# Moving the load of x from SyncE's queue to ScalarE's queue at the start of a decode kernel

## The chip, the core and the metric

The kernel runs on one core of a Trainium2 chip. The metric is the device time of one execution in microseconds. Before the change it is 1309.38 us, the median of three runs that lie between 1309.34 and 1309.76 us. The core has a matrix engine (TensorE, PE in the profile), a vector engine (VectorE, DVE), an activation engine (ScalarE, ACT), GpSimd (POOL), and SyncE (SP), which here only issues transfers. ScalarE can issue transfers too. All transfers run on the same 16 DMA engines; what SP issues appears in the profile as queue q1, what ScalarE issues as queue q10.

## The reference

Eight sequences decode one token each. x is 8 x 512. It is normalised to xn, and three things are added: x itself, grouped-query attention of xn over a cache of 8192 keys and values (8 key heads of width 128, 32 query heads), and a two-layer Mish network of xn (512 to 1792 to 512).

```python
xn = layernorm(x)
q = xn @ wq                       # 8 x 32 heads x 128
p = softmax(q . k_cache / sqrt(128))
attention = (p @ v_cache) @ wo
h = xn @ w1 + b1
out = x + attention + (h * tanh(softplus(h))) @ w2
```

All numbers are 32-bit floats. The caches alone are 8 x 8 x 8192 x 128 x 4 bytes each, 537 MB for the two. Each cached number is used once per query head of its group, so the program is mostly a stream from memory.

## The kernel before

The work is cut into 32 units (`UNITS`). A unit is one sequence and two key heads. It loads one block of keys (`kT`, 128 rows of 64 KB, 8.39 MB) and one block of values (`v`, the same size), each with one transfer from `load_unit` (line 145). Four times, once for eight units, the query weights `wq` of two key heads are loaded into `ws` (2 MB) and multiplied with xn (`project`), and the result is spread over a layout that the scores need (`spread`, `key_weights`).

All these blocks live in one large tile `kv`. One place holds values. Two places for keys overlap each other by half. So the transfers depend on what has been read out before them: the next key block may be issued once the first half of the present scores is done, the next value block once the present value products are done.

The scheduling is by hand (`manual_schedule`): each engine executes its instructions in the order in which the program writes them. SP issues nearly all transfers, in the order of the code, and each issue waits until its place is free. What SP has issued runs one after the other on q1.

The start is special in three ways.

- The first key block goes to the value place and has nothing to wait for. It is issued at once, followed by the Mish weights `w1` (line 573).
- The first 2 MB of `wq` are split: SP issues one half (line 159), ScalarE the other (line 160), so both queues work.
- x lies in a corner of `kv` (`x_sb`, line 154) that the second key place will overwrite. It is normalised by a chain of small instructions on VectorE and ScalarE (lines 209 to 225, ending in `xn4`). `project` needs `xn4` and both halves of `ws`. After `spread` and `key_weights`, `x_turn` (lines 248 to 267) reads `x_sb` once more with TensorE (line 252). Only then may SP issue the second key block, kT(1) (line 578 of the code, line 145 in the profile).

After unit 0's scores, SP issues the first value block v(0) (line 603). Then `mish` runs the first Mish layer, whose scratch and weights lie in the other key place; its last VectorE instruction is line 490. Only then may SP issue the third key block, kT(2). Below, kT(j) and v(j) are the blocks of unit j.

ScalarE issues three more small transfers at the start, the bias `b1` (line 165), then loads its table for the square root and takes part in the normalisation.

Of the kernel before, what the change touches and what calls it, by code (L numbers as in the profile page):

```python
# [82 lines left out]
def kernel(  # L83
# [12 lines left out]
    nc = tc.nc  # L96
# [55 lines left out]
    low = kv[:B, LOW_AT : LOW_AT + 3 * D]  # L152
    xe = kv[:B, LOW_AT + 3 * D : LOW_AT + 3 * D + W1R * P].rearrange("b (i s) -> b i s", i=W1R)
    x_sb, xc, sq = (low[:, i * D : (i + 1) * D] for i in range(3))
    nc.sync.dma_start(x_sb, x)  # L155

    rows = wq.rearrange("j p f -> (j p f)").rearrange("(m p f) -> m p f", m=NP, p=P)[0]
    half = CC * BW // 2
    nc.sync.dma_start(ws[:, :half], rows[:, :half])  # L159
    nc.scalar.dma_start(ws[:, half:], rows[:, half:])  # L160
    b1_sb = kv[:G, W1_AT + 7168 : W1_AT + 7168 + FG]

    for lo in range(0, FG, 150):
# [537 lines left out]
```

## Time and profile before

| | before |
|---|---|
| time, median of 3 runs | 1309.38 us |
| span of the profiled execution, first to last instruction | 1307.7 us |
| TensorE busy | 991.8 us (76%) |
| VectorE busy | 357.6 us (27%) |
| ScalarE busy | 39.2 us (3%) |
| moved by the DMA engines | 561.80 MB, mean 430 GB/s |
| of it on ScalarE's queue q10 | 1.06 MB |

The profiled execution's span is the time from its first to its last instruction. It lies 1.7 us under the median of the runs, which are timed from outside and without a profile. An issue row (SPq, ACTq) is the moment at which an engine hands a transfer to the DMA engines; the data moves later. In the rows "idle before <-X" tells how long an engine stood still before an instruction, and what ended that. The DMA view counts the packets that start in a window, by queue; a packet of this program is one contiguous row of a transfer, or a small mark of 4 bytes with which a DMA engine reports that its share is done.

### The profile page before, as it was taken

What the parts mean: (1) busy time and instruction counts of PE and PEld (TensorE: products, weight loads), DVE (VectorE), ACT (ScalarE), POOL (GpSimd) and SP (SyncE); (2) the same over time, 40 slices, a digit from 0 to 9 for tenths busy, and PEclk for the clock granted to TensorE, in tenths of its full rate; (3) what the DMA queues carried; (4) which work ended last, traced back from release to release, by engine and by line L of the source; (5) the groups of instructions that cost most, each with busy time, mean ns of one, the idle gap of its engine ahead of it and who ended that gap; (6) DMA issues with size and microseconds to landing.
All of it is one profiled execution on the core that took longest, in us unless ns stands there. A gap on an engine that the chain in (4) does not pass through costs nothing.

```text
span 1307.7 us, 11247 instructions
## 1 busy us (share of the span) xinstructions
PE 991.8 (76%) x5090; PEld 348.8 (27%) x5090; DVE 357.6 (27%) x676; ACT 39.2 (3%) x89; POOL 2.3 (0%) x10
## 2 busy tenths in 40 slices
PE   6967876768878778776877877687696687777686
PEld 4222222223322222222322222232242222222222
DVE  3352122231233332123221322311323321323321
ACT  1000000000000000000000000000000000000000
POOL 0000000000000000000000000000000000000000
PEclk9999888888888788888888888798888998888898
DMA  9999999999999999999999999999999999999998
GB/s 404 444 421 442 425 439 428 433 435 430 434 433 432 435 432 436 424 442 429 434 434 429 438 425 442 423 440 427 437 426 436 435 428 436 432 432 429 433 435 337
DMA packets 11927, 561.80 MB, mean 430 GB/s; under 512 B 1364, under 2 KB 1632, under 8 KB 2152
## 3 DMA queue, kind: packets, MB, share of 16 engines
q1 hardware_dynamic: 11712, 560.03, 99.2%
q10 hardware_dynamic: 168, 1.06, 0.3%
q8 instruction: 40, 0.66, 0.2%
q14 instruction: 7, 0.06, 0.0%
HBM read 561.01 MB, written 0.07 MB: 429 GB/s over the span
## 4 chain that ended last, share of the span: by engine, by line
DMA 77%; PE 23%; issue 0%; ACT 0%; SPq 0%; DVE 0%
DMA kv<-in_v 57%; DMA kv<-in_kT 18%; PE o L410 15%; PE s L340 7%; DMA kv<-in_w 2%; PE x L379 1%; PE x L304 0%; ACT qr L311 0%; PE o L564 0%; PE m L427 0%; SPq L155 0%; SPq L159 0%; DVE os L661 0%; DVE rt L387 0%; PE m L383 0%
## 5 line engine op out<-in xcount | busy, mean ns | idle before, releaser
L340 PE MATMUL s<-kv,wk 128*64 128x512 f32 x2048 | 502.8, 654 | 177.0 <-DMA kv<-in_kT 169.9
L410 PE MATMUL o<-kv,pt 128*32 128x512 f32 x2048 | 267.6, 682 | 56.6 <-DMA kv<-in_v 56.6
L340 PEld LDWEIGHTS s<-kv,wk 128*64 128x64 f32 x2048 | 164.0, 151 | 492.1 <-issue 403.5
L352 DVE TENSOR_REDUCE nm<-s 128x1 f32<-128x512 f32 x32 | 22.1, 692 | 511.6 <-PE s L340 511.6
L379 PE MATMUL x<-e,perm 128*128 128x512 f32 x256 | 130.7, 658 | 2.0 <-ACT qr L311 2.0
L410 PEld LDWEIGHTS o<-kv,pt 128*32 128x32 f32 x2048 | 70.5, 123 | 227.8 <-issue 175.1
L418 DVE TENSOR_SCALAR os<-o,isel 128x128 f32<-128x128 f32 x32 | 11.2, 351 | 281.5 <-PE o L410 281.5
L390 DVE STREAM_TRANSPOSE tr<-x 128x512 f32<-128x512 f32 x128 | 79.2, 676 | 3.2 <-PE x L379 3.2
L379 PEld LDWEIGHTS x<-e,perm 128*128 128x128 f32 x256 | 50.6, 208 | 75.5 <-issue 72.9
L323 DVE TENSOR_TENSOR wk<-qr,mask 128x1024 f32<-128x1024 f32 (+1 forms) x33 | 62.8, 1902 | 18.8 <-ACT qr L311 18.7
L371 ACT ACTIVATE e<-s,nmx 128x512 f32<-128x512 f32 x32 | 22.0, 687 | 1115.4 <-DVE nmx L368 1115.4
L399 DVE TENSOR_TENSOR pt<-tr 64x512 f32<-64x512 f32 x64 | 43.9, 686 | 1.6
L395 DVE TENSOR_TENSOR tr<-tr 128x1024 f32<-128x1024 f32 x32 | 39.2, 1225 | 1.1
L420 DVE SCALAR_TENSOR_TENSOR os<-o,isel,os 128x128 f32<-128x128 f32 x96 | 33.7, 351 | 3.4
L353 PE MATMUL m<-ident,nm 128*1 128x128 f32 x32 | 8.6, 270 | 25.3 <-DVE nm L352 25.3
L364 PE MATMUL m<-ident,nx 1*128 1x1 f32 x32 | 7.0, 217 | 19.8 <-DVE nx L358 19.8
L304 PE MATMUL x<-qT,tr 128*128 128x64 f32 x128 | 19.3, 315 | 3.0 <-ACT qr L311 2.7
L304 PEld LDWEIGHTS x<-qT,tr 128*128 128x128 f32 x128 | 18.1, 226 | 6.2 <-ACT qr L311 3.3
L353 PEld LDWEIGHTS m<-ident,nm 128*1 128x1 f32 x32 | 2.5, 79 | 53.5 <-DVE nm L352 53.5
L374 DVE TENSOR_SCALAR lsel<-rsel,l 128x8 f32<-128x8 f32 x32 | 7.4, 231 | 28.8 <-ACT e L371 28.8
L427 PE MATMUL m<-hsel,os 128*128 128x8 f32 x64 | 10.9, 242 | 5.6 <-DVE rt L387 5.6
L427 PEld LDWEIGHTS m<-hsel,os 128*128 128x128 f32 x64 | 10.8, 189 | 15.2 <-DVE rt L387 7.2
(107 smaller groups left out, 174.6 us busy)
## 6 DMA issues: line engine op xcount, KB each, us to landing
ws<-in_wq SPq DMA_DIRECT2D x3, 2048.0 KB
kv<-in_wo SPq DMA_DIRECT2D x2, 2048.0 KB
kv<-in_w SPq DMA_DIRECT2D x1, 3584.0 KB
kv<-in_w SPq DMA_DIRECT2D x2, 1024.0 KB
kv<-in_wo SPq DMA_DIRECT2D x1, 1920.0 KB
kv<-in_wo SPq DMA_DIRECT2D x1, 1536.0 KB
ws<-in_wq ACTq DMA_DIRECT2D x1, 1024.0 KB
ws<-in_wq SPq DMA_DIRECT2D x1, 1024.0 KB
```

The source lines that it names most:

```text
L304: nc.tensor.matmul(X[:, half, k * 64 : (k + 1) * 64], wide[:, half * 8 + k], qT, start=True, stop=True,)
L323: nc.vector.tensor_mul(w[:, i : i + n], q[:, i : i + n].to_broadcast([P, n, 2, NH * G, REP]), mask.rearrange("p (o d k r) -> p o d k r", o ...
L340: nc.tensor.matmul(S[64 * c : 64 * (c + 1), :], w[:, i].rearrange("p d k h -> p (d k h)"), kk[:, i, c, :], start=(part == 0 and n == 0), s ...
L352: nc.vector.tensor_reduce(nm, S, axis=AX.X, op=ALU.max, negate=True)
L371: nc.scalar.activation(e, S, AF.Exp, bias=nmx, accum_out=l)
L379: nc.tensor.matmul(X[:, g], perm[:, g], e, start=True, stop=True)
L390: nc.vector.transpose(tr.rearrange("p (l t) c -> p t l c", t=TL)[:, tl], X.rearrange("p g (t q l) -> p t l g q", t=TL, q=PP)[:, tl],)
L395: nc.vector.tensor_add(t[:, :, 0], t[:, :, 0], t[:, :, 1])
L399: nc.vector.tensor_add(pt8[half, :, :, d * REP : (d + 1) * REP].rearrange("p c y h -> p y c h"), t[:, 0], t[:, 1],)
L410: nc.tensor.matmul(O[Q * q : Q * (q + 1), :], pt8[:, c, TL * l : TL * (l + 1), :].rearrange("p t h -> p (t h)"), vt[:, 512 * n : 512 * (n ...
L420: nc.vector.scalar_tensor_tensor(os, O[:, DH * i : DH * (i + 1)], isel[:, i : i + 1], os, op0=ALU.mult, op1=ALU.add)
L427: nc.tensor.matmul(M[:, 168 : 168 + H2], os, hsel, start=True, stop=True)
```

## The change

The issue of x moves from SP to ScalarE. On SP it was the first transfer, ahead of SP's half of `wq`. On ScalarE it comes right behind ScalarE's half of `wq` and ahead of the three pieces of `b1`.

```diff
     x_sb, xc, sq = (low[:, i * D : (i + 1) * D] for i in range(3))
-    nc.sync.dma_start(x_sb, x)
 
     rows = wq.rearrange("j p f -> (j p f)").rearrange("(m p f) -> m p f", m=NP, p=P)[0]
     half = CC * BW // 2
     nc.sync.dma_start(ws[:, :half], rows[:, :half])
     nc.scalar.dma_start(ws[:, half:], rows[:, half:])
+    nc.scalar.dma_start(x_sb, x)
     b1_sb = kv[:G, W1_AT + 7168 : W1_AT + 7168 + FG]
```

The order of SP's issues at the start of the program, as a difference. `ws<-in_wq` is a half of the query weights, `kv<-in_x` is x, `kv<-in_kT` the first key block, `kv<-in_w` the Mish weights. The code loses a line above, so line 159 reads 158 after the change:

```order
 L696 UNCONDITIONAL_BRANCH
-L155 DMA kv<-in_x 8x512
-L159 DMA ws<-in_wq 128x2048
+L158 DMA ws<-in_wq 128x2048
 L145 DMA kv<-in_kT 128x16384
 L573 DMA kv<-in_w 128x7168
```

SP's half of the weights, the first key block and the Mish weights each move one place forward.

The order of ScalarE's issues at the same place (`kv<-in_b` are the pieces of the bias):

```order
 L696 UNCONDITIONAL_BRANCH
-L160 DMA ws<-in_wq 128x2048
+L159 DMA ws<-in_wq 128x2048
+L160 DMA kv<-in_x 8x512
 L165 DMA kv<-in_b 4x150 x2
 L165 DMA kv<-in_b 4x148
```

x stands behind 1 MB on its queue, and the bias and all of ScalarE's later work stand one issue further back. The other engines' instructions and their order are the same.

## The prediction, made before the changed kernel ran

> **What bounds the kernel now.** I read the page first: the busy times and the line of DMA shares in its 40 slices.
>
> ```profile
> span 1307.7 us, 11247 instructions
> PE 991.8 (76%) x5090; PEld 348.8 (27%) x5090; DVE 357.6 (27%) x676; ACT 39.2 (3%) x89; POOL 2.3 (0%) x10
> DMA  9999999999999999999999999999999999999998
> DMA packets 11927, 561.80 MB, mean 430 GB/s; under 512 B 1364, under 2 KB 1632, under 8 KB 2152
> ```
>
> No engine is near full, but the DMA engines are busy in all 40 slices. 561.80 MB at 430 GB/s is 1306 us, the whole span. So only two things change the time: when the stream starts, and whether it ever runs dry.
>
> Next, the chain of waits in order of time (start, duration, what), whose head holds the edited issue.
>
> ```profile
> 0.73 0.38 SPq L155
> 1.11 0.06 issue
> 1.17 0.37 SPq L159
> 1.54 0.04 issue
> 1.59 26.29 DMA kv<-in_kT
> ...
> 44.91 31.03 DMA kv<-in_v
> ```
>
> The reader is to see that x's issue costs SP 0.38 + 0.06 = 0.44 us, that kT(0) lands at 1.59 + 26.29 = 27.88, and that v(0), issued at 44.91, lands only at 75.94. It queues behind other blocks, so the stream has stock. How much stock matters, because the change makes x later.
>
> **The change, part by part.** The timeline of the first microseconds (start, duration, engine and line, in brackets the idle time before):
>
> ```profile
> 0.73 0.38 ACTq L160 DMA_DIRECT2D ws<-in_wq  x1
> 1.15 1.36 ACTq L165 DMA_DIRECT2D kv<-in_b  x3
> 2.43 0.67 DVE L209 TENSOR_REDUCE st<-kv 8x1 f32<-8x512 f32 x1 [0.33 <-DMA kv<-in_x]
> 2.54 1.28 ACT L208 ACT_TABLE_LOAD   x1 [2.54 <-issue]
> 3.31 0.47 DVE L211 TENSOR_SCALAR kv<-kv,st 8x512 f32<-8x512 f32 x1
> 3.94 0.61 ACT L212 ACTIVATE kv<-kv 8x512 f32<-8x512 f32 x1
> 7.26 0.19 DVE L225 COPY xn<-m 128x32 f32<-128x32 f32 x1 [0.80 <-PE m L224]
> 8.66 1.89 PE L279 MATMUL h<-ws,xn 128*8 128x512 f32 x8 [1.44 <-DMA ws<-in_wq]
> 28.01 16.86 PE L340 MATMUL s<-kv,wk 128*64 128x512 f32 x64 [0.58 <-DMA kv<-in_kT]
> ```
>
> *Issues.* SP loses one issue: its half goes out at 0.73 instead of 1.17, and kT(0) and w1 each 0.44 us earlier. ScalarE gains one of about 0.4 us, so the bias and its table load (1.28 us, from 2.54) begin 0.4 us later. That is covered: the table is needed only at L212, which will itself be late. Without the cover it would cost 0.4 us.
>
> *Is the earlier issue on SP worth anything?* The DMA view of two windows, 0 to 4.7 us and then 4.7 to 7.2 us, and of 8.5 to 20 us (queue: packets, MB, share):
>
> ```profile
> q10 hardware_dynamic: 110, 0.90, 61.9%
> q1 hardware_dynamic: 16, 0.02, 1.5%
> ...
> q1 hardware_dynamic: 111, 0.91, 85.7%
> q10 hardware_dynamic: 56, 0.15, 15.4%
> ...
> q1 hardware_dynamic: 77, 5.05, 101.4%
> ```
>
> Until 4.7 us q1 has moved x alone, though SP's half was issued at 1.17; the engines were busy with ScalarE's half, issued at 0.73 before and after. SP's half followed at once. Whichever half goes first, kT(0) begins after the same 2 MB. The gain lies between 0 and the full 0.44 us; I take 0.1, since the engines are served from the other queue meanwhile.
>
> *When does x come?* Before, it was issued at 0.73 and released L209 at 2.43. Now it stands behind 1 MB on q10, and the other half shares the engines. L279 shows that both halves had landed by 8.66. If ScalarE's half goes first alone, x comes one half sooner: 1.05 MB at 430 GB/s is 2.4 us, so at 6.2. If the halves take turns and x follows directly, at about 8.7. Or it meets kT(0) first. In the third window q1 moves 5.05 MB in 77 packets, 65.6 KB each, a whole row of a key block. One of 16 engines moves 430/16 = 26.9 GB/s, so a row holds its engine 2.44 us. The second window shows that the queues mix: bias packets of q10 are moved amid SP's half. If x's row and the mark that reports it take turns with kT(0)'s rows, each turn costs 2.44 us. With n such turns, x comes at R = 8.7 + 2.44 n.
>
> *What R does to the rest.* From L209 to the end of L225 are 7.45 - 2.43 = 5.02 us, and 0.1 less when L212 finds its table ready. L279 then starts at R + 4.95 instead of 8.66, a shift S = R - 3.7: 2.5 us at R = 6.2, 5.0 at n = 0, 7.4 at n = 1, 9.9 at n = 2. From L279 to the first scores (28.01) each engine waits on the one before; the scores start S later, minus the 0.1 us by which the keys were last. Everything queued behind these on PE and DVE moves with them, and two issues of SP behind that:
>
> ```profile
> 27.54 0.34 SPq L145 DMA_DIRECT2D kv<-in_kT  x1
> ...
> 66.99 0.22 DVE L490 COPY aT<-kv 128x112 f32<-128x112 f32 x1
> 67.28 0.33 SPq L145 DMA_DIRECT2D kv<-in_kT  x1
> ...
> 83.20 0.33 SPq L145 DMA_DIRECT2D kv<-in_v  x1
> ...
> 95.34 15.63 PE L340 MATMUL s<-kv,wk 128*64 128x512 f32 x64 [7.69 <-DMA kv<-in_kT]
> ```
>
> *Where the stream could run dry.* SP issues kT(1) at 27.54, once x_turn has read x, and kT(2) at 67.28, once mish has ended (L490). A transfer moves its first bytes about 1.0 us after its issue: x, issued at 0.73, has 8 packets in the window 1.6 to 1.78 us. For the end of v(0), the window 73.8 to 74.5 us:
>
> ```profile
> DMA packets 8, 0.01 MB, mean 68 GB/s; under 512 B 2, under 2 KB 2, under 8 KB 8
> ...
> DMA packets 24, 0.79 MB, mean 1124 GB/s; under 512 B 12, under 2 KB 12, under 8 KB 12
> ```
>
> Twelve of the 16 engines write their closing mark of v(0) there and start on kT(2); the last is done shortly before the landing at 75.94, say 75.4. So kT(2) must be issued between 72.8 and 74.4, and has 5.5 us (first engines) to 7.1 us (last) to spare. kT(1) must come before w1 has drained: 27.88 + 3.67 MB / 430 GB/s = 36.4 landed, about 34.9 as an issue for the last engine, a spare of some 7. v(0), issued at 44.91, follows kT(1), which lands at 36.4 + 19.5 = 55.9, and has over 9. v(1) at 83.20 comes before kT(2) lands (95.34) with over 10. So kT(2) decides, and the loss is about S - 5.5 to S - 7.1, or nothing. A late kT(1) delays v(0) too, so the two losses are not added: the later one sets the sum. Nothing is won back, as the stream has no idle time to give.
>
> *Sum.* R = 6.2 or 8.7: S is 2.5 or 5.0, no loss, -0.1 us. n = 1: S = 7.4, a loss of 0.3 to 1.9. I take the row nearest to the trace, x behind both halves and behind no row or one, and the middle between no loss and the mean of 1.1: +0.5, less the 0.1 at the start, +0.4 us on the profiled span (1308.1) and on the median: **1309.8 us**, with 1309.2 to 1311.3 as this case's own range.
>
> **The rivals.**
>
> *Turns against key rows (slower).* The place is q10 behind ScalarE's half; the price is 2.44 us per turn, and it decides from S = 5.5 to 7.1 on, that is R above 9.2 to 10.8. x and kT(0) are both the second issue of their engine now, so they reach the engines together. n = 2 gives S = 9.9, a loss of 2.8 to 4.4: 1312.2 to 1313.8. n = 3 gives up to 6.8: 1316.2. If SP's half gets ahead, rows of ScalarE's half meet key rows too, and n is 4 to 7: 7.7 to 16.6 us, 1317 to 1326. For it: the mixing in the second window. Against: in the first window one queue's eight packets per engine went without mixing, and if those are ScalarE's again, x escapes.
>
> *A whole block ahead of x.* The first window can be read as each queue being served in long runs. If SP's half, then ScalarE's, then all of kT(0) goes before x, then R = 8.7 + 19.5 = 28.2, S = 24.5, a loss of 17 to 19: 1327 us. The bias that moved amid SP's half speaks against it. The Trainium skill, DMA: Bandwidth & Descriptors, section "Queues, rings and completion order", has this rule: an engine takes a whole packet, typically 9 to 17 descriptors, from one queue before it turns to the next. By it the sum would be 1327 us if SP's half is first and 1309.3 if ScalarE's is. The first window agrees with it, the second does not.
>
> *The full 0.44 us.* If one queue cannot fill the engines at the start, SP's earlier half fills them: 1308.9. Against it stands the 61.9% that q10 took alone, which leaves little, and a late x cannot help.
>
> **How the numbers follow.** The forecast has 0.48, the full gain 0.10, n = 2 or 3 has 0.22, n of 4 to 7 has 0.12, the whole block 0.08. A measurement of this kernel can tell about 0.2%, 2.6 us, from no change. The forecast and nearly all of the gain case lie within it: same 0.56, with 0.02 for faster. The three slow cases lie beyond it: 0.42. The range reaches from the full gain, 1308.9, to n of 3 and the first of 4, 1317, and leaves out 0.2. The forecast's own range is 1309.2 to 1311.3.
>
> **What would show it.** In the changed profile: SP's half issued near 0.73; L209 released by x between 6 and 11 us, L279 five microseconds later and idle on xn instead of on `ws`; the scores of unit 0 at 28.0 + S; kT(2) issued at 67.3 + S. If R is under 9.2, the DMA row stays full through 80 us and the time is the same. If L209 waits until 13 us or more, the forecast is wrong, and windows of the DMA view near 36 and 75 us must show the gap. If R is small and the time still moves by over 2.6 us, the account of the stream is wrong.

## The result, and the profile after

The changed kernel is slower: 1314.43 us, the median of five runs between 1313.03 and 1315.37, against 1309.34 for the kernel before (five runs between 1309.12 and 1309.76). The ratio is 1.0038, with an interval from 1.0027 to 1.0048, a loss of 5.1 us. The profiled execution spans 1311.9 us against 1307.7. That is 4.2 us more; it is one of the faster executions of the changed kernel. The runs of the changed kernel lie 2.3 us apart, those of before 0.6. Two of the ten runs of an experiment below (x behind SP's half) took 1613 us at a granted clock of 0.56 instead of 0.88, and one of 19 runs of the kernel before took 3264 us; the ratios leave these out.

The start of the changed kernel, from its timeline (start, duration, engine and line, in brackets the idle time before and what ended it):

```profile
0.73 0.42 ACTq L159 DMA_DIRECT2D ws<-in_wq  x1
0.73 0.38 SPq L158 DMA_DIRECT2D ws<-in_wq  x1
1.18 0.42 SPq L145 DMA_DIRECT2D kv<-in_kT  x1
1.19 0.58 ACTq L160 DMA_DIRECT2D kv<-in_x  x1
...
13.39 0.68 DVE L209 TENSOR_REDUCE st<-kv 8x1 f32<-8x512 f32 x1 [11.29 <-DMA kv<-in_x]
18.38 1.90 PE L279 MATMUL h<-ws,xn 128*8 128x512 f32 x8 [0.28 <-DVE xn L225]
37.26 0.34 SPq L145 DMA_DIRECT2D kv<-in_kT  x1
...
76.12 0.33 SPq L145 DMA_DIRECT2D kv<-in_kT  x1
```

SP's half and kT(0) are issued 0.4 us earlier, as written. But x, issued at 1.19, releases L209 only at 13.39 instead of 2.43. L279 begins at 18.38 instead of 8.66, now waiting on xn and not on the weights. kT(1) is issued at 37.26 instead of 27.54, and kT(2) at 76.12 instead of 67.28.

Where x waits is seen in the DMA view. The first pair of rows is the window 0 to 8.5 us of the changed kernel, the second pair 8.5 to 13 us (queue: packets, MB, share of the engines):

```profile
q1 hardware_dynamic: 160, 2.10, 66.0%
q10 hardware_dynamic: 144, 1.05, 30.4%
...
q1 hardware_dynamic: 32, 2.10, 107.6%
q10 hardware_dynamic: 16, 0.02, 1.0%
```

By 8.5 us q10 has moved 144 packets, which are the 128 rows and 16 marks of its half, and nothing of x. The 16 packets of the next window are x: eight rows of 2 KB and eight marks. In the same window q1 moves 32 rows of 64 KB, two on each of the 16 engines. The trace has the order: the first rows of kT(0) start from 7.2 us on, x's rows between 9.6 and 10.5, its marks between 12.1 and 13.0. x's data waits for one row of kT(0), x's mark for the next.

What the late issue of kT(1) does is seen microsecond by microsecond (from:to, then the busy time of each engine, the granted clock, the DMA share and GB/s). First before, then after:

```profile
35.00:36.00 1.00, 1.00 (x7) 0.31 (x4) 0.00 (x0) 0.00 (x0) 0.00 (x0) 1.00 2.34 1012
36.00:37.00 1.00, 1.00 (x8) 0.34 (x6) 0.00 (x0) 0.00 (x0) 0.00 (x0) 1.00 0.15 66
37.00:38.00 1.00, 1.00 (x8) 0.44 (x6) 0.00 (x0) 0.00 (x0) 0.00 (x0) 1.00 1.06 459
38.00:39.00 1.00, 1.00 (x7) 0.31 (x4) 0.00 (x0) 0.00 (x0) 0.00 (x0) 1.00 1.21 524
```

```profile
35.00:36.00 1.00, 1.00 (x8) 0.88 (x8) 0.00 (x0) 0.30 (x1) 0.00 (x0) 1.00 0.01 0
36.00:37.00 1.00, 1.00 (x14) 0.63 (x13) 0.68 (x1) 0.29 (x1) 0.00 (x0) 1.00 0.06 16
37.00:38.00 1.00, 1.00 (x8) 0.30 (x6) 0.96 (x4) 0.00 (x0) 0.00 (x0) 1.00 0.00 0
38.00:39.00 1.00, 1.00 (x6) 0.38 (x4) 0.00 (x0) 0.00 (x0) 0.00 (x0) 1.00 2.88 983
```

A packet counts where it starts, so single rows jump. In the kernel before, rows of kT(1) begin in the first of these microseconds (1012 GB/s), and the stream goes on. In the changed kernel nothing is moved from the end of the Mish weights until 38 us but one fetch of instructions (16 GB/s). SP's issue at 37.26 moves its first bytes about 1.0 us later, at 38.22.

The loss is carried through to the end. The landing of kT(2), seen at the first score of unit 2, is 95.34 before and, in the changed kernel:

```profile
99.36 16.22 PE L340 MATMUL s<-kv,wk 128*64 128x512 f32 x64 [4.17 <-DMA kv<-in_kT]
```

That is 4.0 us later, and the span 4.2 us longer: by unit 2 nearly the whole loss has been made, and nothing later gives it back.

### The profile page after: what moved, and what is told of

Its sections match the earlier page's. It is cut to its first block, busy times and chain, and to the rows that moved or that the text cites. A ratio compares the mean times of both kernels' runs of the same rounds, so it can differ in the third digit from the quotient of the medians.

```text
span 1311.9 us, 11246 instructions
## 1 busy us (share of the span) xinstructions
PE 989.3 (75%) x5090; PEld 347.6 (26%) x5090; DVE 357.6 (27%) x676; ACT 39.3 (3%) x89; POOL 2.3 (0%) x10
## 4 chain that ended last, share of the span: by engine, by line
DMA 73%; PE 26%; DVE 0%; ACT 0%; issue 0%; ACTq 0%
DMA kv<-in_v 54%; DMA kv<-in_kT 16%; PE o L410 15%; PE s L340 8%; DMA kv<-in_w 2%; DMA kv<-in_x 1%; PE x L304 1%; PE x L379 1%; PE h L456 1%; PE h L279 0%; PE m L289 0%; ACT qr L311 0%; DVE nm L352 0%; ACT e L286 0%; PE o L564 0%
## 5 line engine op out<-in xcount | busy, mean ns | idle before, releaser
L410 PE MATMUL o<-kv,pt 128*32 128x512 f32 x2048 | 263.0, 672 | 54.6 <-DMA kv<-in_v 54.6
```

Source lines behind the costliest of these rows:

```text
L410: nc.tensor.matmul(O[Q * q : Q * (q + 1), :], pt8[:, c, TL * l : TL * (l + 1), :].rearrange("p t h -> p (t h)"), vt[:, 512 * n : 512 * (n ...
```

## The experiments

The theory under test has two halves. First, rows of the two queues take turns on each DMA engine, so a small transfer of q10 pays a whole row of q1 per turn. Second, what costs time is not the mixing, but the late issue of kT(1), through xn and x_turn. The rivals are the mixing itself, the order of the two halves, and a queue's whole run going ahead of x.

### x first on ScalarE's queue

```diff
-    nc.scalar.dma_start(ws[:, half:], rows[:, half:])
     nc.scalar.dma_start(x_sb, x)
+    nc.scalar.dma_start(ws[:, half:], rows[:, half:])
```

> The changed kernel, but ScalarE issues x ahead of its half of the query weights, not behind it; SP's half stays its queue's first transfer. Theory (x's place behind the half lets it meet the key rows): L209 is released at about 2.5 us, kT(1) is issued at 27.5 us, the time is that of before within 0.5 us, 1308.9 to 1309.8. Rival (the two halves going out together, or x on ScalarE's queue at all, costs the time): 1313 to 1315 remain. The full gain of 0.44 us from SP's earlier half would show here as 1308.9.

Measured: 1323.73 us, ratio 1.0108 (1.0093 to 1.0123). The expectation missed by 14 us, and the miss taught the most. Of its timeline:

```profile
0.73 0.38 SPq L158 DMA_DIRECT2D ws<-in_wq  x1
1.17 0.42 SPq L145 DMA_DIRECT2D kv<-in_kT  x1
1.34 0.36 ACTq L160 DMA_DIRECT2D ws<-in_wq  x1
2.75 0.67 DVE L209 TENSOR_REDUCE st<-kv 8x1 f32<-8x512 f32 x1 [0.65 <-DMA kv<-in_x]
28.05 1.88 PE L279 MATMUL h<-ws,xn 128*8 128x512 f32 x4 [18.21 <-DMA ws<-in_wq]
46.89 0.33 SPq L145 DMA_DIRECT2D kv<-in_kT  x1
```

x comes at once, but now ScalarE's half is late: it is issued at 1.34, 0.6 us behind SP's half, and lands at 28.05. Its DMA view shows the windows 0 to 4.7 us and 8.5 to 20 us:

```profile
q1 hardware_dynamic: 114, 0.93, 59.1%
q10 hardware_dynamic: 16, 0.02, 1.7%
...
q1 hardware_dynamic: 64, 4.19, 84.1%
q10 hardware_dynamic: 64, 0.52, 10.7%
```

In the first window SP's half goes alone; q10 moves x and nothing else. In the second, 64 rows of 64 KB and 64 rows of 8 KB alternate one to one. So ScalarE's half pays for a key row with each of its rows. This is the kernel before in a mirror. There, x as SP's first transfer held SP's half back by one issue (0.44 us), and ScalarE's half went first and alone. SP's half came second and could lose no turn, because the key rows stand behind it on its own queue.

### x on SP's queue, behind SP's half

```diff
     nc.scalar.dma_start(ws[:, half:], rows[:, half:])
-    nc.scalar.dma_start(x_sb, x)
+    nc.sync.dma_start(x_sb, x)
```

> The changed kernel, but x is issued by SP behind SP's half and ahead of kT(0). x then still waits for a half, but shares a queue with the key rows and takes no turns with them. Theory: L209 is released at 8 to 9 us, so the scores start 4.3 to 5.3 us late, kT(1) is issued at 31.8 to 32.8 us, ahead of the end of the Mish weights, and the time is that of before within 0.5 us. Rival (x behind a half is late enough by itself): 1311 or more.

Measured: 1309.84 us, ratio 1.0004 (0.9994 to 1.0014). The same kernel once more, for its profile:

> x on SP's queue behind SP's half, unedited, for a profile at the usual clock. Theory: L209 at 8.8 us as in the profile at hand, kT(1) issued at about 32.7 us, 5.2 us late and in time, no gap near 36 us, a time of 1309.7 to 1310.1.

Measured: 1309.87 us, span 1308.1. L209 starts at 8.87, kT(1) is issued at 32.74, and the stream goes on (window 34 to 36 us):

```profile
8.87 0.67 DVE L209 TENSOR_REDUCE st<-kv 8x1 f32<-8x512 f32 x1 [6.77 <-DMA kv<-in_x]
...
34.00:36.00 2.00, 2.00 (x6) 0.47 (x4) 0.00 (x0) 0.00 (x0) 0.00 (x0) 1.00 1.63 696
```

x waits for 2 MB of weights here too, and both halves set out together. Being behind a half costs 6.4 us of x's time and 0.4 to 0.7 us of the kernel's. The turns against key rows make the rest.

### kT(0) in short rows first

```diff
-    k_t = {0: load_unit(kT, 0, V_AT)}
+    k0 = kT[:NB].rearrange("j p f -> (j p f)").rearrange("(p f) -> p f", p=P)
+    for lo, hi in ((0, 2048), (2048, ROW)):
+        nc.sync.dma_start(kv[:, V_AT + lo : V_AT + hi], k0[:, lo:hi])
+    k_t = {0: kv[:, V_AT : V_AT + ROW]}
```

> The changed kernel, but kT(0) is issued in two transfers, first its first 2048 columns (rows of 8 KB), then the rest (rows of 56 KB). x's place is that of the changed kernel. Theory (each turn costs one row of the other queue): a turn costs 0.3 us instead of 2.44, L209 is released at 8.7 to 9.5 us, kT(1) is issued at 32.5 to 33.4 us, and the time is that of before within 0.6 us. Rival (x waits for something other than single rows, as for a queue's whole run): L209 stays at 13 us or later and the time at 1313 to 1315.

Measured: 1310.57 us (1310.10 to 1311.62), ratio 1.0009 (0.9999 to 1.0019). x has the place of the changed kernel, and only the rows that it meets are an eighth as long:

```profile
9.13 0.67 DVE L212 TENSOR_REDUCE st<-kv 8x1 f32<-8x512 f32 x1 [7.03 <-DMA kv<-in_x]
33.00 0.34 SPq L145 DMA_DIRECT2D kv<-in_kT  x1
```

L209 (here L212) comes at 9.13 instead of 13.39. By an estimate, a run of all eight short rows would have taken 2.4 us (8 x 8 KB at 26.9 GB/s) and put it past 11; so x waits for single rows, not for a queue's run, and most of the loss is gone. One thing more is different: SP's issue of the Mish weights waits for `ws` until 8.84 us (1.63 in the changed kernel). That is long before kT(0) has landed, so the stream does not notice. The profile shows no gap, yet the time stays 1.1 us above before; that remainder is open.

### A late xn without any mixing

The kernel before, with x loaded first by SP, and fills of a scratch tile ahead of L209.

```diff
+    for _ in range(21):
+        nc.vector.memset(H, 0.0)
     nc.vector.reduce_sum(st[:, 0:1], x_sb, axis=AX.X)
```

> The kernel before with x loaded first by SP, and 21 fills of a scratch tile (0.48 us each) put on VectorE ahead of L209, so that L209 starts at about 13.4 us although x landed at 2.4. The transfers at the start are those of before. Theory (the late xn alone makes the loss, through the late issue of kT(1) and kT(2)): kT(1) is issued at about 37.3 us, the stream is empty for some 2 to 3 us near 36 to 38 us, and the time is that of the changed kernel, 1313 to 1315.4. Rival (the loss comes from the mixing of the queues in the first microseconds): the time of before, 1309.3.

Measured: 1315.62 us, ratio 1.0047 (1.0032 to 1.0062). The fills started 0.67 us apart, though each took 0.48, so L209 (here L211) started at 15.93 and kT(1) was issued at 39.74. The stream is empty (window 36 to 38 us), though the first microseconds are those of before:

```profile
39.74 0.33 SPq L145 DMA_DIRECT2D kv<-in_kT  x1
...
36.00:38.00 2.00, 2.00 (x11) 1.95 (x10) 0.00 (x0) 0.00 (x0) 0.00 (x0) 1.00 0.00 0
```

The late xn alone makes a loss, without any mixing. That it is as large as the changed kernel's is shown by the same with 12 and 16 fills:

> The kernel before with 12 fills of a scratch tile on VectorE ahead of L209, so that L209 starts at about 8.6 us and everything behind it some 4.9 us late. Theory (the stock of the stream covers 5.5 us or more): kT(1) is issued at 32.4 us, no gap, the time of before within 0.4 us. Rival (any delay of the scores costs time): +2 us or more.

> The kernel before with 16 such fills, L209 at about 10.7 us, the rest 7.0 us late. This is one turn's worth. Theory: kT(1) is issued at 34.6 us, its first bytes move at 35.6 us, when most engines have just run out: a loss of 0 to 1.5 us. If the loss grows in proportion to the delay from zero on, it is 3.4 us.

Measured: with 12 fills, L209 at 9.93 and kT(1) at 33.73, 1311.87 us (ten runs, 1309.82 to 1313.25), ratio 1.0016 (1.0006 to 1.0025), more than expected. With 16, L209 at 12.60 and kT(1) at 36.40, 1313.35 us (1312.22 to 1315.59), ratio 1.0032 (1.0020 to 1.0044). As the fills lay further apart, both delays are larger than meant: 6.2 us instead of 4.9, and 8.9 instead of 7.0. The changed kernel, issuing kT(1) at 37.26, lies between 16 and 21 fills in this and in its time. By its number alone, 12 fills gave what the rival expected (2 us or more), and the three losses (2.5, 4.0 and 6.1 us) would also fit a loss in proportion to the delay. Against that rival stands x behind SP's half: kT(1) is 5.2 us late there, and the loss is 0.4 to 0.7 us, where proportion would give about 2.

### More turns

```diff
-    nc.scalar.dma_start(x_sb, x)
+    for lo in (0, D // 2):
+        nc.scalar.dma_start(x_sb[:, lo : lo + D // 2], x[:, lo : lo + D // 2])
```

> The changed kernel, but x goes in two transfers of 256 columns on ScalarE's queue, so that two rows and two marks take turns with kT(0)'s rows. Theory: four turns, L209 is released at about 18.2 us, kT(1) is issued at about 42.1 us, the stream is empty from about 35.5 to 43 us, a loss of 7.5 to 10 us: 1317 to 1319. Rival (the wait does not go by turns): L209 at 13.4 us as in the changed kernel, 1313 to 1315.

Measured: 1319.85 us, ratio 1.0080 (1.0063 to 1.0097). L209 (here L210) starts at 18.18, forecast 18.2: two turns more than 13.39 make 4.79 us, 2.40 each. kT(1) is issued at 42.04. The time is 0.9 us above the expected range. The trace shows a second gap: kT(2) is issued at 82.27, and no row starts between 82 and 83 us.

```diff
     nc.scalar.dma_start(ws[:, half:], rows[:, half:])
-    nc.scalar.dma_start(x_sb, x)
...
         nc.scalar.dma_start(b1_sb[:, lo:hi], b1.rearrange("(g f) -> g f", g=G)[:, lo:hi])
+    nc.scalar.dma_start(x_sb, x)
```

> The changed kernel, but ScalarE issues x behind the three pieces of the bias. Four engines carry bias pieces: three rows and three marks more on their queue. Theory: eight turns on these, so x lands behind nearly all of kT(0)'s eight rows, L209 at 25 to 28 us, a loss of 14 to 19 us: 1324 to 1328. Rival (the wait does not go by turns): L209 near 13.4 us, 1313 to 1315.

Measured: 1327.50 us, one run. L209 starts at 28.04, a little past the expected 25 to 28. kT(1) is issued at 51.90, and this is the stream from 36 to 50 us:

```profile
36.00:50.00 14.00, 12.24 (x55) 10.16 (x55) 3.57 (x18) 1.17 (x2) 0.00 (x0) 1.00 0.00 0
```

### Why the runs scatter

> The changed kernel once more, unedited, to see another execution: its runs lie 2.3 us apart (1313.03 to 1315.37), those of before 0.6. Theory: the scatter is the halved clock of TensorE during the first Mish layer. In the profiles so far the time from the issue of v(0) to that of kT(2) is 20.7, 22.4 or 24.1 us, with 0, about 3 and about 6 us at half clock in it. The first gap, from a kT(1) issued at 37.3 us, is the same each time, 2.7 us. With 20.7 or 22.4 us the span is 1311 to 1312; with 24.1 kT(2) is issued near 77.8 us, about 1.5 us after the place where v(0) runs out, and the span is 1313 to 1314. Rival (slower rows of the key blocks after the gap): the span varies with the interval unchanged.

> The changed kernel a third time, unedited, with the same expectations: 20.7 or 22.4 us from the issue of v(0) to that of kT(2) goes with a span of 1311 to 1312, 24.1 us with 1313 to 1314.

> The kernel before with 12 fills ahead of L209, unedited: its ten runs lie between 1309.8 and 1313.3. Theory: kT(1) is issued at 33.7 us each time, without a gap; the time goes by the interval from v(0)'s issue at about 49 us to kT(2)'s. With 20.7 us the span is 1308 to 1309, with 22.4 us up to 1309, with 24.1 us 1309 to 1311. Rival (kT(1) at the edge makes the scatter): a gap near 35 to 37 us in a slow execution.

Measured, with the issue times from the timelines and all spans from the profiled executions:

| execution | kT(1) issued | v(0) issued | kT(2) issued | v(0) to kT(2) | span |
|---|---|---|---|---|---|
| changed, second | 37.25 | 52.86 | 73.56 | 20.70 | 1311.2 |
| changed, first | 37.26 | 53.76 | 76.12 | 22.36 | 1311.9 |
| changed, third | 37.11 | 53.81 | 76.18 | 22.37 | 1313.2 |
| 12 fills, first | 33.73 | 49.06 | 69.76 | 20.70 | 1308.4 |
| 12 fills, second | 33.73 | 50.46 | 72.83 | 22.37 | 1310.6 |

The clock that was granted during the first Mish layer, in the second and third execution of the changed kernel (the third column from the right):

```profile
57.80:59.80 2.00, 2.00 (x28) 0.63 (x24) 0.12 (x1) 0.00 (x0) 0.00 (x0) 1.00 1.21 524
```

```profile
57.80:59.80 2.00, 2.00 (x16) 0.47 (x12) 1.07 (x1) 0.00 (x0) 0.00 (x0) 0.50 1.21 524
```

At clock 0.50 TensorE does 16 instead of 28 products in the same two microseconds. The interval grows by 1.67 us, kT(2) is issued 2.6 to 3.1 us later, and the span is 0.7 to 2.2 us longer. The direction is as expected, the size is not: an interval of 22.4 us went with 1311.9 in one execution and with 1313.2 in another, although I expected it to cost nothing; with 12 fills it went with 1310.6 instead of up to 1309; and 24.1 us did not occur among these five.

The microseconds in which kT(2) begins show what the late issue does, in the second and then in the third execution of the changed kernel:

```profile
77.00:78.00 1.00, 1.00 (x8) 0.34 (x6) 0.88 (x3) 0.00 (x0) 0.00 (x0) 1.00 2.12 918
78.00:79.00 1.00, 1.00 (x6) 0.14 (x2) 0.65 (x1) 0.00 (x0) 0.00 (x0) 1.00 0.15 66
```

```profile
77.00:78.00 1.00, 1.00 (x8) 0.37 (x6) 1.00 (x3) 0.00 (x0) 0.00 (x0) 1.00 1.04 393
78.00:79.00 1.00, 1.00 (x6) 0.29 (x4) 0.97 (x2) 0.00 (x0) 0.00 (x0) 1.00 1.12 393
```

In the second execution 15 rows of 64 KB start (984 GB/s in all), and each holds its engine for 2.42 us (2.27 x 16 / 15). In the third only 12 start, and each takes 2.88 us: the stream ran dry again. From the packets of the traces, the engines stand still 0.65 us on average between 77 and 79 us in the third execution, and not at all in the first and second. With 12 fills they stand still 0.44 us between 73 and 77 us in the second execution, and not in the first. The kernel before has the dip in its profile too, with 5.5 us to spare at kT(2), and its runs scatter by 0.6 us only. So the dip can bring kT(2) too late for the stream; that it makes the whole scatter of the unprofiled runs is likely, not shown.

## Why the prediction was right and where it was wrong

The time, 1314.43 us, lies in the range on record (1308.9 to 1317.0). The forecast itself, no change at 1309.8, did not come. What came is the first rival, turns against key rows with n = 2, which the range took in with a chance of 0.22 for n = 2 or 3. The mechanism was written down, but as a rival, and not as the forecast.

- **The step that failed** is the choice of n: "x behind both halves and behind no row or one". Measured: L209 at 13.39 us, R = 8.7 + 2 x 2.35, two turns. The rival's paragraph held the reason, that x and kT(0) are now both the second issue of their engine. The issues are 0.01 us apart (1.18 and 1.19), and after equal halves the turns begin with a key row; that these 0.01 us decide which comes first was not tested. The mixing of the queues was in the second window that I quoted. I gave the first window as much weight, where one queue went alone, and did not ask why it did. The experiment with x first on ScalarE's queue answers that: the half that is issued ahead (by 0.61 us there, by 0.44 in the kernel before) fills the engines first.
- **The price of a turn**, 2.44 us by 430 GB/s over 16 engines and 65.6 KB, held: 2.40 us between the changed kernel and x in two pieces.
- **The shift** S = R - 3.7 held: R = 13.39 gives 9.7, and L279 moved from 8.66 to 18.38, 9.72 us; kT(1) moved by the same 9.72.
- **The spare times** were about right, and the place was partly wrong. I wrote that kT(2) decides. In the profile the gap stands at kT(1), between 35 and 38 us. From the executions: with kT(1) issued at 33.73 (12 fills, first execution) kT(2) landed 0.3 us late, with 36.40 it was 2.8 us late (98.13 against 95.34). So its spare time is between 6.2 and 8.9 us; in the changed kernel, 9.7 us late with a gap of 2.7, it comes to 7.0, against the 7 forecast. kT(2) is issued 8.8 us late (76.12 against 67.28), but the gap at kT(1) has already moved v(0) back: its first row starts at 58.1 instead of 54.5. So kT(2) needs only about 5.2 of its own spare time and is near its limit of 5.5 to 7.1. The two limits lie close together; I took the wrong one for the first.
- **The size** for n = 2, a loss of 2.8 to 4.4 us, compares with 4.2 in the profiled execution and 5.1 in the median. That it came so near is in part luck: it was worked out for a gap at kT(2). The gap at kT(1) is 2.7 us, and two terms were missing. The first rows after the gap take longer, which adds 0.6 us (below), and the executions scatter, the three profiled ones from 1311.2 to 1313.2, where kT(2) has no spare time left.
- **The earlier issue on SP** was worth nothing that can be seen, as forecast: kT(0) is issued 0.4 us earlier and its rows follow the same 2 MB. x first on SP, which the chain of waits showed as 0.44 us of cost, cost the kernel nothing: it put SP's half behind ScalarE's, and both still passed before the key rows, as they also do when issued together.
- **The whole block ahead of x** falls: by it, L209 would have come at 28 us in the changed kernel. The rule of the Trainium skill, DMA: Bandwidth & Descriptors, section "Queues, rings and completion order", that an engine drains a packet of typically 9 to 17 descriptors from one queue before turning to the next, does not agree with this case's traces: in the kernel with x first on ScalarE, 64 rows against 64 rows between 8.5 and 20 us are four and four on each engine, and the trace has them 16 and 16 in every 2.7 us, one of each per engine.

All kernels in one table. They differ in what mixes at the start, but the time rises with the issue of kT(1) from row to row:

| kernel | L209 starts | kT(1) issued | first score of unit 2 | time, us |
|---|---|---|---|---|
| before | 2.43 | 27.54 | 95.34 | 1309.34 |
| x behind SP's half | 8.87 | 32.74 | 95.83 | 1309.84 |
| short key rows first | 9.13 | 33.00 | 95.85 | 1310.57 |
| 12 fills | 9.93 | 33.73 | 95.62 | 1311.87 |
| 16 fills | 12.60 | 36.40 | 98.13 | 1313.35 |
| changed | 13.39 | 37.26 | 99.36 | 1314.43 |
| 21 fills | 15.93 | 39.74 | 101.83 | 1315.62 |
| x in two pieces | 18.18 | 42.04 | 105.62 | 1319.85 |
| x first on ScalarE | 2.75, `ws` at 28.05 | 46.89 | 110.10 | 1323.73 |
| x behind the bias | 28.04 | 51.90 | 113.84 | 1327.50 |

The first three columns are of one profiled execution, the time is the median. From 36.40 on, each microsecond of later issue is about a microsecond of time (15.5 us of issue, 15.7 of landing, 14.2 of time from 16 fills to x behind the bias). No version is faster than before. x behind SP's half is the one that equals it.

## What to carry to other kernels

A small load on a second queue was not free of the first queue's traffic: here it paid one row of the other queue for its data and one for its mark, so its wait was set by the length of the rows that it met (2.4 us each for 64 KB). Put small, early-needed loads ahead of large rows on the same queue, or let the first transfers beside them have short rows. Before taking an issue off the head of the chain of waits, ask which transfer it had been letting pass.

## What was not expected

- The order of two equal transfers on two queues was decided by 0.44 to 0.6 us of issue time, and decided 14 us of the kernel: 1309.34 with ScalarE's half ahead, 1323.73 with SP's half ahead. When both were issued at 0.73, they went in turns, and L279 found both landed.
- After a gap the stream loses more than the gap. In the changed kernel the engines close the Mish weights between 35.1 and 36.0 us and move again from 38.2 on, a gap of 2.7 us on the average of the 16; the first score of unit 2 is 4.0 us late. In the second execution, where kT(2) was issued early enough (73.56), it is still 3.8 us late (99.12). Some 0.6 us of the difference stands in the rows above: between 38 and 39 us of the changed kernel 15 rows start (983 GB/s), and each holds its engine for 3.07 us (2.88 x 16 / 15), against 2.42 (1.21 x 16 / 8) in the kernel before. Rows that start between 40 and 57 us take 2.42 us again. Why the first ones take longer, and where the last half microsecond goes, stays open.
- A fill of 128 x 512 numbers on VectorE took 0.48 us, but fills of the same tile in a row started 0.67 us apart.
